# A planner's costs, seven exponential slots, and later loads in a two-layer attention and token-mixing kernel

## The chip, the cores and the metric

The kernel runs on one core of one Trainium2 chip. The metric is the device time of one execution in microseconds, the median of several runs. The profile is that of one execution; its times are counted from the first instruction of the span.

The core has five engines with a queue of instructions each: TensorE (PE) multiplies matrices and writes PSUM; VectorE (DVE), ScalarE (ACT) and GpSimd (POOL) work on tiles in SBUF and, the first two, in PSUM; SyncE (SP) issues DMAs. POOL issues two small DMAs as well. Engines wait for each other by semaphores only.

## The reference

Two kinds of blocks take turns, twice over, on x of 2048 tokens by 512 features in bfloat16.

```python
x = x + A(layernorm(x))     # attention over a sliding window
x = x + B(layernorm(x))     # a perceptron across the tokens
x = x + A(layernorm(x))
x = x + B(layernorm(x))
```

A projects to queries, keys and values (wqkv, 512 by 1536), for 32 heads of 16 features. A token attends to itself and the 255 tokens before it: scores times 1/4, masked, softmax, product with the values, and the output projection wo (512 by 512). B normalises its input once more, multiplies over the tokens with w1 (2048 by 1792), adds b1, applies the tanh form of gelu, multiplies with w2 (1792 by 2048) and adds b2. Both layers use the same weights.

## The kernel before

**Tiles.** Tokens come in 16 tiles of 128 (x_sb, and normalised xh_sb). Attention works on four quarters Q of 512 tokens. For a quarter, xhT holds the transposed normalised tokens (two buffers); k_sb, q_sb and v_all hold projections, doubled with zeros for two half sets of heads, so that small matmuls of 64 by 64 tiles can serve several heads at once. The zeros are made in `masked` (line 464 on DVE, 469 on ACT) as the projection leaves PSUM.

**Steps of attention.** A quarter has 4 groups of heads by NB = 9 shifts: 36 steps, 144 in a layer, 288 in all. A step is `emit_scores` (line 581, PE), `emit_exp` (line 592, one exponential on ACT from a pair of PSUM banks to a slot of p_sb, then one or two small multiplications with the triangles in `edge`, line 609, on POOL or DVE), and `emit_pv` (line 630, PE: the product with the values, which accumulates over the nine shifts in two PSUM banks). p_sb has NSLOT = 5 slots, taken in turn; the scores have two pairs of banks. The table `v_all` also holds ones, which make the denominators in the same product. Every second group the denominators are gathered by small DMAs into den_c, inverted (`job_inverse`), spread back over the heads by a product with the 0/1 table `spread` (`job_normalise`, line 674) and multiplied in; then comes wo (`job_outproj`, line 548) with the addition to x_sb and the statistics of the next normalisation.

**Beside the steps.** Projections (`job_k`, `job_q`, `job_v`: lines 454 and 500) of the later head groups and of the next quarter, the transposes of the next quarter, the output projection of the last quarter, and parts of the token products run between the steps of a quarter. They take their banks in turn from two (`misc_bank`). The transposes of the very first quarter are matmuls with the identity (line 443); all others are DMAs from SP (line 435).

**Token products.** `u_product` (line 752) multiplies w1 with the tokens in groups of four matmuls for each quarter of the tokens, and `job_y` (line 789) multiplies w2 in two halves of ten and four matmuls. Twelve of the sixteen output tiles of the first layer's second product are laid over the attention of the second layer.

**The order.** Nothing is ordered by hand on the engines. Every operation is entered with `plan.op`: the engines that may do it and its cost in ns on each, the resources that it reads and writes, a place `prio`, and `lat`, the time that its successors wait after its end (80 by default, 200 for PE). `Plan.arrange` walks through simulated time; an engine that is free takes, of the operations that are ready within 60 ns, the one with the lowest place (PE adds STAY = 1.0 to the place of one that would change its tile mode between "full", "columns" and "cells", and SWITCH = 100 ns to its time). A DMA ends at the end of its issue or of the bus, plus its bytes at 200 per ns, plus 1600. The order found is fixed in the program; `emit` writes it out with semaphore waits. Between two operations of PE no wait is written. Places are in units of which a quarter has 20: step n of a layer has place base + 5n/9, its scores and exponential 1.0 less, its value product 1.6 more.

**What the change touches.** `XPOS`, `XSTEP`: the places of the four loads of tokens 8 to 15 (256 KB each, tiles 8-9, 10-11, 12-13, 14-15) and, two further steps, of the two halves of wo (256 KB each); each waits by `after=latest` for the exponential that was entered last before it. `XLAT`: the additional latency of a DMA transpose. `constants`: the ones of three blocks of v_all (line 384, POOL), then spread (a memset, line 831, and sixteen selections, line 838), then the DMAs of the two bias vectors from POOL (line 844), which read spread as their time to start. `warm`: 13 groups of ten matmuls into one bank at the start (line 394). `first_norm`: the normalisation of a quarter of the input (statistics line 400, DVE; lines 408 to 420).

Of the kernel before, what the change touches and what calls it, by code (L numbers as in the profile page):

```python
# [13 lines left out]
FIRSTV = -0.7  # L14
# [5 lines left out]
XPOS = 0.7  # L20
XSTEP = 1.2
NORM0 = 6.5
XLAT = 1500
# [16 lines left out]
class Plan:  # L40
# [53 lines left out]
    def arrange(self):  # L94
# [13 lines left out]
        while todo:  # L108
# [40 lines left out]
            for s in o.succ:  # L149
                s.left -= 1  # L150
                s.ready = max(s.ready, o.end + (0 if e == "tensor" and e in s.on else o.lat))
                if not s.left:
                    for x in s.on:
                        pool[x].append(s)
# [80 lines left out]
def bass_interleave_layers__sliding_block__mixer_token_mlp__prompt_kernel(  # L235
# [20 lines left out]
    NSLOT = 5  # L256

    es = ExitStack()
    with es:
# [171 lines left out]
        def job_transpose(Q, i, prio):  # L431

            t, buf = 4 * Q + i, Q % 2
            if prio > 0:
                plan.op({SP: (600, lambda e: e.dma_start_transpose(xhT[:, buf, :, i * P:(i + 1) * P], xh_sb[:, t, :]))},
                        reads=[R("xh", t)], writes=[R("xhT", buf, i)], prio=prio, dma=1 << 17, lat=XLAT)
                return
# [21 lines left out]
        def masked(b, prio, dst, src, mask, key, writes):  # L459
# [11 lines left out]
            plan.op({ACT: (1380, each)} if key == "even" and prio < 0 else {DVE: (MASKED, both), ACT: (1380, each)}, reads=[R(key)], shares=[BK(b)], writes=writes, prio=prio)  # L471
# [37 lines left out]
        def first_jobs(p0, dp):  # L509
# [3 lines left out]
                    [(p0 + 9 + FIRSTV + 0.3 * i, lambda p, i=i: job_v(0, i, p)) for i in range(4)])  # L513

        def span_jobs(Q, p0):
# [3 lines left out]
            beside = {"q1": (0, 1), "q2": (2,), "k3": (3,)} if Q + 1 < NQ else {}  # L519
            if Q == 0:  # L520
                order = [j for j in order if j[0] != "o"]
# [162 lines left out]
        def attention(L, base):  # L684
            todo, n = [], 0
            for Q in range(NQ):
# [9 lines left out]
                todo += span_jobs(Q, base + 20 * Q)  # L696
# [114 lines left out]
        for n, a in enumerate(range(8, 16, 2)):  # L811
            todo.append((XPOS + XSTEP * n, lambda p, a=a: load_x(a, a + 2, p, after=latest)))
        for n in range(2):
            todo.append((XPOS + XSTEP * (n + 4), lambda p, n=n: load(
# [7 lines left out]
        for g in range(NQ):  # L822
            todo.append((-20 if g == 0 else 18 * g - 19, lambda p, g=g: first_norm(g, p)))

        def constants(p):
            for n in range(2, 5):
                for i in range(2):
                    put_ones(n, i, p + 5 * n, [R("xh", 3)], (POOL,))

# [21 lines left out]
        for L in range(2):  # L851
# [24 lines left out]
            for st in range(NT):  # L876
                p, b = base + 131 + st, st % 6
                if L == 0 and 4 <= st < 8:
                    p = BASE - 9 + 2.2 * (st - 4)
                elif L == 0 and st >= 8:  # L880
                    p = BASE + (8 + 3 * (st - 8) if st < 12 else 26 + 3 * (st - 12))
                    b = None
# [35 lines left out]
```

## Time and profile before

| what | value |
| --- | --- |
| median of three runs | 533.8 us (533.21 to 535.61) |
| the profiled execution | 534.36 us, its span 532.6 us |
| PE busy | 484.0 us, 91% |
| PEld (weight loads, beside PE) | 273.7 us |
| DVE, ACT, POOL busy | 318.7, 296.1, 234.4 us |
| granted TensorE clock, mean | 0.997 |
| moved by DMA | 44.38 MB, 83 GB/s |

Stages in the span: up to 13 us the first loads, normalisation and transposes; 13 to 180 us attention of layer one with parts of its first token product; 180 to 225 us the rest of that product; 225 to 248 us the first part of the second one; 248 to 437 us attention of layer two, with the rest of the second product laid over it; 437 to 530 us both token products of layer two.

How to read it: a row of the timeline has start, length, engine, line, operation, output and inputs, the number of instructions, and in brackets how long the engine was idle before and what ended that. "issue" stands where nothing that the profile shows ended it. A row of the table by stretches has, for each engine, busy time and instructions, then the granted clock of PE, the mean share of the 16 DMA engines and GB/s. A row of waits has who waited for whom, the total, the number and the longest. In the DMA view a row has a queue, its packets, MB, and the time of its packets as a share of 16 engines; packets that stand in line count while they stand, so it can pass 100%. q0 are POOL's DMAs, q1 those of SP, q8 fetches instructions.

### The profile page before, as it was taken

To read this page: it belongs to the slowest core of one execution; us is meant where nothing else is said; L and a number is where in the kernel's file an instruction comes from. 1 tells how busy PE (TensorE), PEld (TensorE's weight loads), DVE (VectorE), ACT (ScalarE), POOL (GpSimd) and SP (SyncE) were. 2 spreads that over 40 slices of the span, in tenths; PEclk is the share of its full clock that TensorE was granted. 3 is DMA by queue.
4 is the path that set the end of the run, shared out by engine and by line. 5 is a ranking of instruction groups with operands and counts; after the bars stand their busy time and mean duration, and the time that the engine had idled before them with its cause. 6 is when DMAs were issued, how large, how long until landed. Compare 5 with 4: busy or idle time off the path is not lost.

```text
span 532.6 us, 21297 instructions
## 1 busy us (share of the span) xinstructions
PE 484.0 (91%) x9540; PEld 273.7 (51%) x9618; DVE 318.7 (60%) x539; ACT 296.1 (56%) x335; POOL 234.4 (44%) x468
## 2 busy tenths in 40 slices
PE   7779889989889899999889888988998989999997
PEld 7455555655555444445545555555645544444443
DVE  5778869868767361157756767596876655221222
ACT  5757887988888304300746766479888860230000
POOL 5976864756665301101735644276565540200000
PEclk9999999999999999999999999999999999999999
DMA  6192515210135430533203410032221635053631
GB/s 198 45 121 66 103 44 97 72 45 25 45 96 158 124 108 0 138 103 78 43 3 94 105 31 25 3 53 73 83 65 57 192 113 149 1 140 97 180 113 44
DMA packets 84443, 44.38 MB, mean 83 GB/s; under 512 B 20864, under 2 KB 83328, under 8 KB 84352
## 3 DMA queue, kind: packets, MB, share of 16 engines
q1 hardware_dynamic: 80480, 43.00, 30.7%
q0 software_dynamic: 3872, 0.02, 1.9%
q8 instruction: 75, 1.23, 1.0%
q14 instruction: 16, 0.13, 0.1%
HBM read 32.51 MB, written 2.10 MB: 65 GB/s over the span
## 4 chain that ended last, share of the span: by engine, by line
PE 72%; DVE 12%; issue 7%; POOL 5%; ACT 3%; SPq 1%; DMA 0%; POOLq 0%; ACTq 0%; DVEq 0%
PE ps L789 18%; PE ps L752 18%; PE ps L581 9%; PE ps L454 8%; PE ps L630 8%; PE ps L548 5%; PE ps L500 4%; ACT p_sb L592 3%; DVE q_sb L464 2%; POOL p_sb L609 2%; DVE k_sb L464 1%; DVE xh_sb L417 1%; DVE oU L319 1%; POOL rstd L410 1%; PE ps L674 1%
## 5 line engine op out<-in xcount | busy, mean ns | idle before, releaser
L592 ACT ACTIVATE p_sb<-ps 128x1024 bf16<-128x1024 f32 (+8 forms) x288 | 261.3, 972 | 104.1 <-PE ps L581 96.3
L609 POOL TENSOR_TENSOR p_sb<-p_sb,edge 128x128 bf16<-128x128 bf16 (+2 forms) x361 | 171.8, 480 | 137.5 <-ACT p_sb L592 126.2
L581 PE MATMUL ps<-q_sb,k_sb 64*64 64x288 bf16 (+8 forms) x2816 | 106.9, 251 | 10.7 <-ACT p_sb L592 5.4
L630 PE MATMUL ps<-p_sb,v_all 64*64 64x288 bf16 (+8 forms) x2816 | 94.9, 248 | 11.1 <-POOL p_sb L609 6.0
L581 PEld LDWEIGHTS ps<-q_sb,k_sb 64*64 64x64 bf16 x2816 | 54.1, 106 | 60.5 <-ACT p_sb L592 29.7
L630 PEld LDWEIGHTS ps<-p_sb,v_all 64*64 64x64 bf16 x2816 | 58.4, 107 | 27.5 <-POOL p_sb L609 15.6
L793 DVE SCALAR_TENSOR_TENSOR x_sb<-ps,b2col,x_sb 128x512 bf16<-128x512 f32 x32 | 24.0, 750 | 76.0 <-PE ps L789 75.9
L454 PE MATMUL ps<-xhT,wqkv 128*128 128x512 bf16 x216 | 58.2, 384 | 9.8 <-issue 7.4
L789 PE MATMUL ps<-uT,w1buf 128*128 128x512 bf16 x274 | 61.8, 379 | 1.3 <-DVE rc L658 0.8
L464 DVE TENSOR_TENSOR k_sb<-ps,half 128x1024 bf16<-128x1024 f32 x32 | 39.0, 1218 | 16.1 <-PE ps L454 16.0
L752 PE MATMUL ps<-xh_sb,w1buf 128*128 128x512 bf16 x182 | 43.3, 379 | 2.0 <-issue 0.6
L400 DVE BATCH_NORM_STATS2 stats<-x_sb 128x6 f32<-128x512 bf16 x64 | 43.5, 688 | 1.1
L789 PEld LDWEIGHTS ps<-uT,w1buf 128*128 128x128 bf16 x280 | 26.8, 98 | 33.4 <-issue 1.8
L464 DVE TENSOR_TENSOR v_all<-ps,even 128x1024 bf16<-128x1024 f32 x29 | 35.1, 1217 | 11.5 <-PE ps L500 10.9
L464 DVE TENSOR_TENSOR q_sb<-ps,even 128x1024 bf16<-128x1024 f32 x31 | 37.7, 1217 | 4.5 <-PE ps L454 4.3
L410 POOL TENSOR_TENSOR rstd<-vare,mhalf 128x4 f32<-128x4 f32 x16 | 16.2, 1014 | 50.5 <-DVE nmean L412 50.4
L500 PE MATMUL ps<-wqkv,xhT 128*32 128x128 bf16 x2048 | 34.7, 220 | 3.7 <-issue 2.6
L789 PE MATMUL ps<-uT,oU 128*128 128x512 bf16 x165 | 36.8, 379 | 0.2
L454 PEld LDWEIGHTS ps<-xhT,wqkv 128*128 128x128 bf16 x256 | 20.5, 98 | 30.3 <-issue 7.8
L500 PEld LDWEIGHTS ps<-wqkv,xhT 128*32 128x32 bf16 x2048 | 29.1, 97 | 9.9 <-issue 7.2
L779 ACT ACTIVATE uT<-ps,b1col 128x512 bf16<-128x512 f32 x20 | 13.3, 689 | 36.8 <-PE ps L752 36.8
L548 PE MATMUL ps<-wo_sb,oT 128*128 128x512 bf16 x117 | 29.9, 380 | 2.9 <-DVE oT L681 1.7
(67 smaller groups left out, 396.2 us busy)
## 6 DMA issues: line engine op xcount, KB each, us to landing
w1buf<-in_B_w_dram SPq DMA_DIRECT2D x10, 896.0 KB
oU<-in_B_w_dram SPq DMA_DIRECT2D x6, 896.0 KB
w1buf<-in_B_w_dram SPq DMA_DIRECT2D x10, 512.0 KB
oU<-o SPq DMA_DIRECT2D x16, 256.0 KB
k_sb<-in_B_w_dram SPq DMA_DIRECT2D x16, 256.0 KB
xhT<-in_B_w_dram SPq DMA_DIRECT2D x8, 256.0 KB
q_sb<-in_B_w_dram SPq DMA_DIRECT2D x8, 256.0 KB
out_dram<-x_sb SPq DMA_DIRECT2D x16, 128.0 KB
```

Source lines behind the costliest of these rows:

```text
L400: dve(lambda e: e.bn_stats(stats[:, t, :], x_sb[:, t, :]), 690, prio, reads=[R("x", t)], writes=[R("stats", t)])
L454: last = e.matmul(ps[:, b, :], lhsT=wqkv[:, c, c0:c0 + P], rhs=xhT[:, buf, c, :], start=(c == 0), stop=(c == 3))
L464: return e.tensor_tensor(dst, src.unsqueeze(2).to_broadcast([P, n, 2, w]), mask[:].unsqueeze(1).unsqueeze(3).to_broadcast([P, n, 2, w]), o ...
L500: last = e.matmul(acc[32 * a:32 * a + 32, k], lhsT=xhT[:, buf, c, t0:t0 + 32], rhs=wv[:, c, :, a, :], start=(k == 0 and c == 0), stop=(k = ...
L548: last = e.matmul(ps[:, b, :], lhsT=oT[:, buf, t, i * P:(i + 1) * P], rhs=wo_sb[:, t, :], start=(t == 0), stop=(t == 3))
L581: last = e.matmul(ps[64 * c:64 * c + 64, 2 * half + r, 32 * i0:32 * i1], lhsT=k_sb[rows, ring, t, kb % 16, :], rhs=q_sb[rows, t, c, 32 * i ...
L592: latest[0] = plan.op({ACT: (170 + int(2 * (512 - c0) * 0.84), lambda e: e.activation(p_sb[:, slot, :, c0:512], ps[:, 2 * half:2 * half + ...
L609: return e.tensor_tensor(v, v, g, op=ALU.mult)
L630: last = e.matmul(ps[64 * r:64 * r + 64, B_O + (c ^ r), 32 * i0:32 * i1], lhsT=v_all[rows, col:col + 64], rhs=p_sb[rows, slot, r, 32 * i0: ...
L752: r = e.matmul(ps[:, b, :], lhsT=blk[:, n, (ft % 2) * P:(ft % 2 + 1) * P], rhs=xh_sb[:, 4 * g + n, :], start=(first and g == quarters[0] a ...
L789: r = e.matmul(ps[:, b, :], lhsT=blk[:, fc, (st % 2) * P:(st % 2 + 1) * P], rhs=uT[:, fc, :], start=(fc == 0), stop=(fc == NFT - 1))
L793: dve(lambda e: e.scalar_tensor_tensor(x_sb[:, st, :], ps[:, b, :], b2col[:, st:st + 1], x_sb[:, st, :], op0=ALU.add, op1=ALU.add), 750, prio,
```

## The change

- The loads of tokens 8 to 15 get the places 4, 9, 14, 20 (before 0.7, 1.9, 3.1, 4.3), the halves of wo 17 and 23 (before 5.5 and 6.7).
- In the walk, the successors of a PE operation now wait its latency of 200 ns on PE too; before they waited none there.
- NSLOT goes from 5 to 7.
- A DMA transpose costs SP 1230 ns in the plan (before 600), and its additional latency of 1500 goes; the common 80 stays.
- In `constants`, spread and the biases get a place 10 later (SPREADP).
- Constants become names: FIRSTV, VACT, NORM1, YP and ORDER1 have the values that stood in the code before, or leave a branch unused.

```diff
--- before.py
+++ after.py
@@ -11,16 +11,21 @@
 P = 128
 EARLY = 1.0
 PV_LAG = 1.6
-FIRSTV = -0.7
+FIRSTV = (-0.7, -0.4, -0.1, 0.2)
+VACT = 0
+NORM1 = -1
+SPREADP = 10
+ORDER1 = None
+BES1 = {"q3": (0, 1, 2, 3)}
+YP = ((-9, 2.2), (8, 3), (26, 3))
 WARM = 13
 NPART = 4
 PARTQ = (0, 1)
 UP0, UPD = 0.5, 5.0
 MASKED = 1215
-XPOS = 0.7
-XSTEP = 1.2
+XPOS = (4, 9, 14, 20)
+WOPOS = (17, 23)
 NORM0 = 6.5
-XLAT = 1500
 SPAN0 = 0.3
 SPAN = 19.0
 
@@ -148,7 +153,7 @@
             todo -= 1
             for s in o.succ:
                 s.left -= 1
-                s.ready = max(s.ready, o.end + (0 if e == "tensor" and e in s.on else o.lat))
+                s.ready = max(s.ready, o.end + o.lat)
                 if not s.left:
                     for x in s.on:
                         pool[x].append(s)
@@ -253,7 +258,7 @@
     NFT = F // P
     EPS = 1e-5
     SMSCALE = 1.0 / math.sqrt(DH)
-    NSLOT = 5
+    NSLOT = 7
 
     es = ExitStack()
     with es:
@@ -432,8 +437,8 @@
 
             t, buf = 4 * Q + i, Q % 2
             if prio > 0:
-                plan.op({SP: (600, lambda e: e.dma_start_transpose(xhT[:, buf, :, i * P:(i + 1) * P], xh_sb[:, t, :]))},
-                        reads=[R("xh", t)], writes=[R("xhT", buf, i)], prio=prio, dma=1 << 17, lat=XLAT)
+                plan.op({SP: (1230, lambda e: e.dma_start_transpose(xhT[:, buf, :, i * P:(i + 1) * P], xh_sb[:, t, :]))},
+                        reads=[R("xh", t)], writes=[R("xhT", buf, i)], prio=prio, dma=1 << 17)
                 return
             b = misc_bank()
             pv = ps[:, b, :].bitcast(dt.bfloat16)
@@ -468,7 +473,7 @@
                 for h in range(2):
                     last = e.activation(dst[:, :, h], src, ACTF.Copy, scale=mask[:, h:h + 1])
                 return last
-            plan.op({ACT: (1380, each)} if key == "even" and prio < 0 else {DVE: (MASKED, both), ACT: (1380, each)}, reads=[R(key)], shares=[BK(b)], writes=writes, prio=prio)
+            plan.op({ACT: (1380, each)} if key == "even" and prio < VACT else {DVE: (MASKED, both), ACT: (1380, each)}, reads=[R(key)], shares=[BK(b)], writes=writes, prio=prio)
 
         def job_k(Q, t, prio):
 
@@ -510,13 +515,16 @@
 
             jobs = [lambda p, i=i: job_transpose(0, i, p) for i in range(4)] + [lambda p: job_k(0, 0, p), lambda p: job_q(0, 0, p)]
             return ([(p0 + dp * n, job) for n, job in enumerate(jobs)] +
-                    [(p0 + 9 + FIRSTV + 0.3 * i, lambda p, i=i: job_v(0, i, p)) for i in range(4)])
-
-        def span_jobs(Q, p0):
+                    [(p0 + 9 + FIRSTV[i], lambda p, i=i: job_v(0, i, p)) for i in range(4)])
+
+        def span_jobs(Q, p0, L):
 
 
             order = ["k1", "q1", "v0", "v1", "k2", "q2", "v2", "o0", "k3", "q3", "o1", "v3", "K0", "Q0", "o2", "o3"]
             beside = {"q1": (0, 1), "q2": (2,), "k3": (3,)} if Q + 1 < NQ else {}
+            if L == 1 and ORDER1:
+                order = ORDER1.split()
+                beside = {} if Q + 1 == NQ else BES1
             if Q == 0:
                 order = [j for j in order if j[0] != "o"]
             if Q == NQ - 1:
@@ -693,7 +701,7 @@
                         todo.append((p0, step))
                         todo.append((p0 + PV_LAG, lambda p, a=(Q, t, m, n % NSLOT): emit_pv(*a, p)))
                         n += 1
-                todo += span_jobs(Q, base + 20 * Q)
+                todo += span_jobs(Q, base + 20 * Q, L)
             end = base + 20 * NQ
             todo.append((end + 3, lambda p: job_inverse(NQ - 1, p)))
             for t in range(2):
@@ -808,10 +816,10 @@
         BASE = 400
         todo = []
 
-        for n, a in enumerate(range(8, 16, 2)):
-            todo.append((XPOS + XSTEP * n, lambda p, a=a: load_x(a, a + 2, p, after=latest)))
+        for p0, a in zip(XPOS, range(8, 16, 2)):
+            todo.append((p0, lambda p, a=a: load_x(a, a + 2, p, after=latest)))
         for n in range(2):
-            todo.append((XPOS + XSTEP * (n + 4), lambda p, n=n: load(
+            todo.append((WOPOS[n], lambda p, n=n: load(
                 wo_sb[:, 2 * n:2 * n + 2], A_wo.rearrange("(fc p) e -> p fc e", p=P)[:, 2 * n:2 * n + 2], 1 << 18, p, after=latest,
                 writes=[R("wo", n)])))
 
@@ -820,12 +828,13 @@
                 ln_stats(t, p)
             ln_apply(g, False, p)
         for g in range(NQ):
-            todo.append((-20 if g == 0 else 18 * g - 19, lambda p, g=g: first_norm(g, p)))
+            todo.append((-20 if g == 0 else 18 * g - 18 + NORM1, lambda p, g=g: first_norm(g, p)))
 
         def constants(p):
             for n in range(2, 5):
                 for i in range(2):
                     put_ones(n, i, p + 5 * n, [R("xh", 3)], (POOL,))
+            p += SPREADP
 
 
             setup(lambda e: e.memset(spread[:], 0.0), 530, reads=[R("xh", 3)], writes=[R("spread")], prio=p)
@@ -875,11 +884,10 @@
                         todo.append((base + 126, lambda p, n=n, i=i: put_ones(n, i, p, engines=(POOL,), writes=[R("v", n, i, h) for h in range(2)])))
             for st in range(NT):
                 p, b = base + 131 + st, st % 6
-                if L == 0 and 4 <= st < 8:
-                    p = BASE - 9 + 2.2 * (st - 4)
-                elif L == 0 and st >= 8:
-                    p = BASE + (8 + 3 * (st - 8) if st < 12 else 26 + 3 * (st - 12))
-                    b = None
+                if L == 0 and st >= 4:
+                    p0, dp = YP[st // 4 - 1]
+                    p = BASE + p0 + dp * (st % 4)
+                    b = None if p >= BASE else b
                 todo.append((p, lambda p, st=st, b=b, L=L: job_y(st, misc_bank() if b is None else b, L, p)))
         todo.sort(key=lambda v: v[0])
         for p, job in todo:
```

## The prediction

> **What bounds the kernel now.** The page comes first: who is busy, and which chain ends last.
>
> ```profile
> span 532.6 us, 21297 instructions
> PE 484.0 (91%) x9540; PEld 273.7 (51%) x9618; DVE 318.7 (60%) x539; ACT 296.1 (56%) x335; POOL 234.4 (44%) x468
> ...
> PE 72%; DVE 12%; issue 7%; POOL 5%; ACT 3%; SPq 1%; DMA 0%; POOLq 0%; ACTq 0%; DVEq 0%
> ```
>
> TensorE is the bound: 484.0 of 532.6 us. The change takes no matrix work away, so all it can win lies in the other 48.6 us, and in clock lost after long pauses. The table by stage says where these are: the two long token products (180 to 248 and 437 to 530 us) are full to within 2 us, the first 13 us miss 2.6, the end 2.9; the rest, some 41 us, is holes in the two attention stages. "issue" on the chain (7%) is the largest kind: waits that no semaphore explains. The longest is in the first layer; the table of engine time by microsecond shows it (PE first, then weight loads, DVE, ACT, POOL; after them the granted clock):
>
> ```profile
> 33.00:34.00 1.00, 1.00 (x37) 0.83 (x40) 1.00 (x2) 0.93 (x2) 0.85 (x3) 1.00 7.54 12
> ...
> 37.00:38.00 1.00, 0.00 (x0) 0.00 (x0) 0.39 (x1) 0.00 (x0) 0.43 (x2) 1.00 0.53 170
> 38.00:39.00 1.00, 0.00 (x0) 0.00 (x0) 0.00 (x0) 0.00 (x0) 0.00 (x0) 1.00 0.07 14
> 39.00:40.00 1.00, 0.76 (x2) 0.13 (x2) 0.00 (x0) 0.00 (x0) 0.00 (x0) 0.58 0.00 1
> 40.00:41.00 1.00, 1.00 (x17) 0.67 (x20) 0.68 (x1) 0.10 (x1) 0.00 (x0) 0.50 0.07 16
> ```
>
> All engines stand, and the clock falls to half. In the timeline PE stops between two matmuls of one projection, where the code has no wait at all:
>
> ```profile
> 36.28 0.38 PE L454 MATMUL ps<-xhT,wqkv 128*128 128x512 bf16 x1 [0.16 <-issue]
> 39.24 1.04 PE L454 MATMUL ps<-xhT,wqkv 128*128 128x512 bf16 x2 [2.58 <-issue]
> ```
>
> So PE lacked instructions, not data. The DMA view agrees. From 31 to 36.5 us there is no packet of the instruction queue q8, but these:
>
> ```profile
> q0 software_dynamic: 3819, 0.02, 184.2%
> q1 hardware_dynamic: 729, 0.69, 59.8%
> ```
>
> and in 36.5 to 39 us one of q8:
>
> ```profile
> q8 instruction: 1, 0.02, 2.8%
> ```
>
> q0 carries the two bias vectors as 3,872 tiny packets; q1 carries tokens 12 to 15 and wo, which SP issued from 29.0 to 33.4 us. One block of instructions came late behind both.
>
> Next POOL's timeline from 18 to 29 us. It is never idle after 19.7, and every second entry builds the table spread:
>
> ```profile
> 22.95 0.39 POOL L838 TENSOR_SCALAR_AFFINE_SELECT spread<-spread 128x128 bf16<-128x128 bf16 x1
> 23.32 0.33 POOL L609 TENSOR_TENSOR p_sb<-p_sb,edge 128x64 bf16<-128x64 bf16 x1
> 23.60 0.35 POOL L838 TENSOR_SCALAR_AFFINE_SELECT spread<-spread 128x128 bf16<-128x128 bf16 x1
> ```
>
> Last the waits over the whole span (total us, times, longest):
>
> ```profile
> ACT p_sb L592 <- PE ps L630: 5.8, 6, 1.5
> ...
> PE ps L630 <- POOL p_sb L609: 6.0, 17, 1.0
> ...
> PE ps L581 <- ACT p_sb L592: 5.4, 18, 0.5
> ```
>
> The first is an exponential waiting for one of the five slots; the others are PE waiting for masks and for exponentials. They are short.
>
> **The change part by part.** The sum goes against the profiled execution, 534.36 us (span 532.6); the median of the runs is 533.8, 0.56 lower. FIRSTV, VACT, NORM1, YP and ORDER1 at their values give the same places as before: nothing.
>
> *Start.* The walk now puts 200 ns between two PE operations that depend on each other. The 13 warm-up groups write one bank, so the planned warm-up grows by 12 x 0.2 = 2.4 us, and some groups fall behind the first transposes. On the chip no wait goes with it. PE warms from 1.43 to 10.56 us (0.70 per group) and the first transpose starts at 10.40, though the first normalised tile was ready at about 8.96 (half of DVE's pair that begins at 8.59). Won at most 1.4; lost at most one group put ahead of the first projection, 0.7. I take -0.8: the fourth tile is only ready at 9.80, so not all of 1.4 comes through.
>
> *POOL and DVE from 13 to 28 us.* Spread's 17 steps get 10 units more, so the masks go first. Eleven of its steps lie after 19 us: 11 x 0.35 = 3.9 us. Tokens 8 and 9 come later too, and take their statistics (1.27 + 0.3 us) off DVE at 25.7. PE's waits in 13 to 26 us that are neither the start nor instructions are 0.9 + 0.5 + 0.5 + 0.3 + 0.2 = 2.4. But the first product with values waits for the last value tile, which DVE copies at 23.41 after the normalisation; spread is not in that chain. So a third: -0.8. Bounds: -2.4, and +1.3 if one bias issue (1.31 us on POOL) now stands before the masks.
>
> *The stall at 36.66.* Loads wait for exponentials 7, 16, 25 and 35 (x) and 30 and 41 (wo), instead of 1 to 12. Counted in the trace these end at about 27.5, 35.1, 48, 56, 52 and 61 us. So 1 MB leaves the stretch around 33, and the biases, behind spread, go some microseconds later. The stall costs 2.58 us; the half clock after it makes the 16 + 16 score and value matmuls take 1.04 + 0.96 where 0.54 + 0.49 is seen at 44.5, and two projections about 0.7 more: 0.97 + 0.7 = 1.7. Together 4.3. The tiny packets stay, and the 1.01 us stall at 73.38 shows what one block of instructions costs beside a single 0.5 MB load. I take 4.3 - 1.0: -3.3. Bounds -4.3 and 0. [...]
>
> *Where the moved loads are needed.* Tokens 14 and 15 land near 59 us; the normalisation of their group runs on DVE and POOL at 65 to 70. wo lands near 64 and is first read at 82.07 (line 548). Price 0, hidden behind exponentials; without that cover PE would wait the difference, about 3 us. On SP nothing urgent stands behind these loads: the transposes of the second quarter get free of four loads at 26.5 to 31.8, those at 55.0 may get a load before them (0.4 us).
>
> *Seven slots.* The scores of a step are placed 2.6 units before its values, 4.7 steps, so five slots bind now and then and seven do not. Bounds: 0, and -5.8 (all of ACT's wait). From 62 to 142 us PE is busy 71.9 and ACT 67.9 of 80, so most of ACT's wait is covered by PE: a quarter, -1.5.
>
> *PE's latency elsewhere.* Two value products that follow each other are now parted in the plan by whatever else is ready, often a filler (projection 0.87, half of a token product up to 2.17 us). On the chip the work is the same; each added change from 64x64 to full tiles costs 0.16 us (the gap before most L454). Bounds: -2, if scores come forward to ACT, and +7.7, if one step in six of the 288 gets a change more. I take +0.4, two or three changes: the walk had such choices before. In the long token products chains interleave, but PE waits for nothing there: 0; if a gelu became the last thing before the second product, one ACTIVATE, 0.69.
>
> *Transposes.* SP is now charged 1230 ns (the trace: 1238 median) and nothing above the common latency, so the planned landing comes 4.36 - 3.57 = 0.8 us earlier. The first user is planned 1.2 units, some 2.6 us, behind. No wait row of PE shows a late one today. 0; with the cover gone 0.8 for each of 6 groups, 4.7.
>
> Sum: -0.8 - 0.8 - 3.3 - 1.5 + 0.4 = -6.0: 528.4 on the profiled scale, 527.8 against the median.
>
> **The rivals.** *The order gets worse.* With 39 changes of 0.16 us on the chain now, 48 more cost 7.7. In 102 to 112 us ACT is busy 9.77 of 10, so a score that a filler delays is not caught up there. From 38 added changes on, the 6.0 above are eaten; with the early gains at half (-3.0) and all 7.7 lost it ends at 538.5. For it: nearly every value product depends on the one before. Against: PE must do the fillers anyway, and each needs one of two banks and a DVE copy of 1.2 us first.
>
> *The stall moves.* The biases, issued some microseconds later, meet the next block as they do now; only the small terms remain, and seven slots win nothing: 533.8 - 1.6 + 0.4 = 532.6, within what can be told. For it: the 3,872 packets stay, and a block is due about every 4 us. Against: from 36 us on, the megabyte beside them moved at 200 to 340 GB/s until the block came, and it is gone.
>
> *Instructions arrive ahead anyway.* If a deep store of instructions hides the block and PE stood for something else, the 4.3 stay as they are and the rest gives 533.8 - 2.7 = 531.1. [...] Against it: no row names another cause, and PE stood inside one operation.
>
> **How the numbers follow.** The forecast has 0.58, the worse order 0.27, the moved stall 0.10, the hidden block 0.05. Measurements of this kernel lie 533.2 to 535.6 us, so about 0.5% (2.7 us) can be told from no change. Faster takes nearly all of the forecast and half of the last: 0.60; the same 0.15 (the moved stall and rest); slower 0.25. The forecast's own range is 522.5 to 531: below lie the lower ends of start, POOL and stall with half of the slots' 5.8 (1.4 + 2.4 + 4.3 + 2.9 = 11.0, 522.8). The full range reaches into the worse order, to 540.
>
> **What would show it.** PE without a pause over 1.2 us from 30 to 45 us, and clock 1.00 there; x and wo issues single, from 27 to 62 us; masks ahead of spread from 19 us; the first transpose near 9.5; ACT's wait for L630 gone; 0.16 us changes to full tiles on the chain still about 40. It is wrong if PE's holes from 62 to 180 and 260 to 437 us grow by more than 3 us, or a stall over 2 us stands beside the bias packets.

## The result and the profile after

The changed kernel takes 537.49 us (median of 20 runs, 532.56 to 542.48); the kernel before, beside it, 534.34 us (20 runs, 533.21 to 536.2). The ratio is 1.0049, 95% interval 1.0032 to 1.0066: slower by half a per cent, where 1.1% faster (6.0 us) was forecast. The runs of the changed kernel spread over 10 us, those before over 3; that spread turns out to be part of the answer. The longest, 542.48 us, counts as a slow run and stands outside the ratio.

The profiled execution of the changed kernel took 539.37 us, its span 537.6 us, its mean granted clock 0.990 (before 0.997). First the page of the kernel after: busy times, then the chain by engine.

```profile
span 537.6 us, 21374 instructions
PE 498.1 (93%) x9618; PEld 276.9 (51%) x9618; DVE 318.2 (59%) x541; ACT 297.7 (55%) x337; POOL 234.3 (44%) x465
...
PE 77%; DVE 7%; issue 5%; POOL 4%; ACT 4%; DMA 1%; SPq 0%; POOLq 0%; ACTq 0%; DVEq 0%
```

PE's busy time seems to have grown by 14 us, but no matrix work was added. Read the counts first: before, 9,540 matmuls stand beside 9,618 weight loads; after, 9,618 beside 9,618. The profile of before lacks 78 records of matmuls, and what they took is missing from its busy time. Busy PE can't be compared between these two; the starts of the exponentials can.

The stretch that was to gain, in the table by stretches of the kernel after (PE, PEld, DVE, ACT, POOL; granted clock; DMA share; GB/s), with two later stretches:

```profile
32.00:38.00 6.00, 5.93 (x177) 3.57 (x168) 5.25 (x7) 4.84 (x8) 5.00 (x13) 1.00 1.14 52
38.00:44.00 6.00, 5.92 (x173) 3.72 (x167) 5.86 (x10) 4.82 (x8) 4.83 (x14) 1.00 0.29 79
56.00:62.00 6.00, 3.79 (x80) 2.19 (x79) 3.77 (x5) 2.42 (x4) 2.00 (x3) 0.79 0.76 87
...
300.00:310.00 10.00, 7.68 (x228) 5.11 (x220) 5.45 (x12) 8.29 (x9) 7.13 (x12) 0.83 0.33 80
360.00:370.00 10.00, 7.83 (x200) 4.76 (x192) 7.21 (x9) 5.82 (x7) 5.37 (x10) 0.83 0.29 86
```

From 32 to 44 us PE is full and the clock whole: the stall of 2.58 us and its half clock are gone. Now PE loses 2.2 of 6 us at 56 us and 2.2 to 2.3 of 10 at 300 and 360 us, and in each the clock falls. Before, it was halved once, at 39.2 us; here three times, at 59.5, 305.3 and 366.7 us. What this does to the lead is seen in the starts of the exponentials, counted in both traces (us):

| exponential | before | after | after - before |
| --- | --- | --- | --- |
| 0 | 17.74 | 17.94 | +0.20 |
| 9 | 28.80 | 27.24 | -1.56 |
| 18 | 40.90 | 36.07 | -4.83 |
| 27 | 49.67 | 43.89 | -5.78 |
| 36 | 56.98 | 52.14 | -4.84 |
| 45 | 67.01 | 66.09 | -0.92 |
| 63 | 88.89 | 87.44 | -1.45 |
| 144 (first of layer two) | 252.85 | 252.71 | -0.14 |
| 189 | 310.19 | 310.25 | +0.06 |
| 198 | 322.50 | 325.39 | +2.89 |
| 225 | 364.80 | 368.92 | +4.12 |
| 252 | 393.90 | 399.88 | +5.98 |
| 287 (last) | 433.20 | 438.13 | +4.93 |

The forecast gain of some 6 us is there by exponential 27. It is given back in two places: nearly four of the 5.8 us between 52 and 66 us, and six from 310 to 400 us.

The first place in PE's timeline of the kernel after:

```profile
55.26 0.84 PE L505 MATMUL ps<-wqkv,xhT 128*32 128x128 bf16 x45
58.31 0.46 PE L505 MATMUL ps<-wqkv,xhT 128*32 128x128 bf16 x19 [2.21 <-issue]
58.70 0.41 PE L589 MATMUL ps<-q_sb,k_sb 64*64 64x128 bf16 x12
59.05 1.49 PE L459 MATMUL ps<-xhT,wqkv 128*128 128x512 bf16 x4
```

This is the old stall at a new place: PE stops within one projection, for 2.21 us, for nothing that a semaphore explains. The next projection takes 1.49 us where 1.02 was seen at 11.85: half clock. SP's timeline ahead of it and the DMA view of 53 to 56 us (packets, MB, share of 16 engines) show what the block of instructions met:

```profile
52.52 0.54 SPq L318 DMA_DIRECT2D w1buf<-in_B_w_dram  x1
53.16 0.53 SPq L318 DMA_DIRECT2D x_sb<-in_A_x_dram  x1
53.77 2.52 SPq L440 DMA_TRANSPOSE xhT<-xh_sb  x2
```

```profile
q1 hardware_dynamic: 1208, 0.60, 69.6%
q8 instruction: 1, 0.02, 2.2%
```

The one packet of q8 starts at 55.89, when PE has 0.2 us of instructions left, and takes 1.07 us; PE is back 1.35 us after its end. Counted back 128.5 weight loads from the stall (the spacing of such stalls, counted further down), PE entered the block before it at 53.65, so the fetch started 2.25 us after that. The same at 71.5 us: a w1 load of 512 KB issued at 68.07, the packet 2.69 us after the block was entered, and a stall of 2.12 us. PE ate these two blocks, by that count some 128 weight loads with their matmuls each, in 2.5 and 2.9 us.

The waits of PE in the kernel after (total us, times, longest):

```profile
PE ps L589 <- issue: 7.8, 7, 2.1
PE ps L589 <- ACT p_sb L600: 7.4, 19, 0.7
PE ps L505 <- issue: 4.4, 6, 2.2
PE ps L638 <- POOL p_sb L617: 3.9, 12, 0.6
PE ps L638 <- issue: 2.3, 2, 1.3
PE ps L638 <- DVE o L324: 2.3, 5, 0.9
```

Waits for masks fell from 6.0 to 3.9 us, those for exponentials rose from 5.4 to 7.4, and "issue", read here as lack of instructions, is the largest kind with 14.5 us.

### The profile page after: what moved, and what is told of

Read it like the earlier page. It is cut to its first block, busy times and chain, and to the rows that moved or that the text cites. A ratio compares the mean times of both kernels' runs of the same rounds, so it can differ in the third digit from the quotient of the medians.

```text
span 537.6 us, 21374 instructions
## 1 busy us (share of the span) xinstructions
PE 498.1 (93%) x9618; PEld 276.9 (51%) x9618; DVE 318.2 (59%) x541; ACT 297.7 (55%) x337; POOL 234.3 (44%) x465
## 3 DMA queue, kind: packets, MB, share of 16 engines
q0 software_dynamic: 3872, 0.02, 1.1%
## 4 chain that ended last, share of the span: by engine, by line
PE 77%; DVE 7%; issue 5%; POOL 4%; ACT 4%; DMA 1%; SPq 0%; POOLq 0%; ACTq 0%; DVEq 0%
PE ps L760 18%; PE ps L797 18%; PE ps L589 11%; PE ps L638 9%; PE ps L459 9%; PE ps L556 6%; PE ps L505 5%; ACT p_sb L600 4%; POOL p_sb L617 2%; DMA oU<-o 1%; PE ps L682 1%; DVE o L324 1%; DVE q_sb L469 1%; DVE stats L405 1%; POOL rstd L415 1%
## 5 line engine op out<-in xcount | busy, mean ns | idle before, releaser
L617 POOL TENSOR_TENSOR p_sb<-p_sb,edge 128x256 bf16<-128x256 bf16 (+2 forms) x357 | 169.8, 480 | 141.9 <-ACT p_sb L600 131.6
L589 PE MATMUL ps<-q_sb,k_sb 64*64 64x288 bf16 (+8 forms) x2816 | 111.8, 252 | 15.9 <-issue 7.8
L638 PE MATMUL ps<-p_sb,v_all 64*64 64x288 bf16 (+8 forms) x2816 | 107.0, 252 | 10.5 <-POOL p_sb L617 3.9
L589 PEld LDWEIGHTS ps<-q_sb,k_sb 64*64 64x64 bf16 x2816 | 56.1, 107 | 59.9 <-ACT p_sb L600 33.3
L638 PEld LDWEIGHTS ps<-p_sb,v_all 64*64 64x64 bf16 x2816 | 60.4, 109 | 33.3 <-POOL p_sb L617 17.0
L459 PE MATMUL ps<-xhT,wqkv 128*128 128x512 bf16 x256 | 67.1, 387 | 1.7 <-DVE v_all L469 0.7
L797 PE MATMUL ps<-uT,w1buf 128*128 128x512 bf16 x280 | 63.6, 379 | 0.0
L760 PE MATMUL ps<-xh_sb,w1buf 128*128 128x512 bf16 x192 | 45.4, 380 | 0.1
L469 DVE TENSOR_TENSOR k_sb<-ps,half 128x1024 bf16<-128x1024 f32 x31 | 37.6, 1214 | 8.0 <-PE ps L459 7.9
L797 PE MATMUL ps<-uT,oU 128*128 128x512 bf16 x168 | 36.7, 379 | 0.0
L556 PE MATMUL ps<-wo_sb,oT 128*128 128x512 bf16 x128 | 32.3, 381 | 0.5 <-DVE oT L689 0.5
```

What stands on the lines that cost most here:

```text
L459: last = e.matmul(ps[:, b, :], lhsT=wqkv[:, c, c0:c0 + P], rhs=xhT[:, buf, c, :], start=(c == 0), stop=(c == 3))
L469: return e.tensor_tensor(dst, src.unsqueeze(2).to_broadcast([P, n, 2, w]), mask[:].unsqueeze(1).unsqueeze(3).to_broadcast([P, n, 2, w]), o ...
L556: last = e.matmul(ps[:, b, :], lhsT=oT[:, buf, t, i * P:(i + 1) * P], rhs=wo_sb[:, t, :], start=(t == 0), stop=(t == 3))
L589: last = e.matmul(ps[64 * c:64 * c + 64, 2 * half + r, 32 * i0:32 * i1], lhsT=k_sb[rows, ring, t, kb % 16, :], rhs=q_sb[rows, t, c, 32 * i ...
L617: return e.tensor_tensor(v, v, g, op=ALU.mult)
L638: last = e.matmul(ps[64 * r:64 * r + 64, B_O + (c ^ r), 32 * i0:32 * i1], lhsT=v_all[rows, col:col + 64], rhs=p_sb[rows, slot, r, 32 * i0: ...
```

## The experiments

Each run was compared with the kernel before on the same chip; "times" are medians, ratios carry 95% intervals. Two theories at first: the loads, moved, now collide elsewhere; or the order got worse through the latency rule.

### Each part alone

On the kernel before, only the new places of the loads:

```diff
-XPOS = 0.7
-XSTEP = 1.2
+XPOS = (4, 9, 14, 20)
+WOPOS = (17, 23)
...
-            todo.append((XPOS + XSTEP * n, lambda
+            todo.append((p0, lambda
```

> The kernel before with the new places of the x and wo loads alone. Blocks theory (PE stands where a block of instructions is fetched beside heavy loads, and the clock halves after it): the stall of 2.6 us near 37 us goes, and 3 to 5 us are won up to exponential 27; whether they are kept depends on the next load that meets a block: 529 to 534. Order theory (the loads are innocent, the new order of PE is what costs): faster by 3 to 5 us to the end, about 530.

537.06 us, ratio 1.0051 [1.0028, 1.0075]: slower, alone, and outside what either theory expected. PE and DVE in its timelines, then SP's:

```profile
70.30 0.41 PE L581 MATMUL ps<-q_sb,k_sb 64*64 64x192 bf16 x10
72.74 0.20 PE L581 MATMUL ps<-q_sb,k_sb 64*64 64x32 bf16 x2 [2.04 <-issue]
...
94.73 0.41 PE L630 MATMUL ps<-p_sb,v_all 64*64 64x288 bf16 x8 [2.15 <-DVE agg L401]
```

```profile
93.89 0.69 DVE L319 COPY o<-ps 128x512 f32<-128x512 f32 x1 [2.91 <-DMA oU<-o]
```

```profile
88.99 0.40 SPq L313 DMA_DIRECT2D w1buf<-in_B_w_dram  x1
89.48 0.73 SPq L313 DMA_DIRECT2D oU<-o  x1
```

The stall at 36.7 us is gone here too (0.36 us left), and exponential 27 comes 1.97 us earlier. Then PE stops twice. The first stop, 2.04 us with half clock at 73.8 us after it, stands at the block of instructions where the kernel before lost 1.01 us. The second, of 2.15 us, is no lack of instructions: the transfer of o2 to oU is issued behind a 512 KB w1 load on SP and lands 0.6 us after it, at 93.77 us; DVE waits 2.91 us for it before it can empty a value bank again, and PE for DVE. No moved load is issued in the 5 us before either stop; the order around them changed. From exponential 72 on the kernel is 0.9 to 2.4 us late.

On the kernel before, spread and the biases ten later:

```diff
                     put_ones(n, i, p + 5 * n, [R("xh", 3)], (POOL,))
+            p += 10
```

> The kernel before with spread and the biases 10 places later, alone. Blocks theory: the megabyte of x and wo stays together with the bias packets, so a stall of about 2.5 us stays between 33 and 42 us, and the rest is a microsecond at most: 533 to 535. Rival (the tiny packets alone make the stall): it moves with the bias packets and keeps its length; also 533 to 535, but the stall lies beside them wherever they are.

531.54 us, 0.9951 [0.9929, 0.9973]: faster. The megabyte of x and wo stayed where it was (issued from 28.4 to 33.2 us), the biases moved (issued at 31.43 and 33.15 us, before at 28.85 and 30.17), and no stall over 1 us stands near 37 us. Both theories had expected one. Taking either the megabyte or the biases away removes the stall. The other traces agree: at this block PE stands for instructions 1.49 to 3.13 us in all five kernels that keep both (before, s_lat, s_slots, s_transp, q_before) and at most 0.4 us in the other twelve.

On the kernel before, only the latency:

```diff
-                s.ready = max(s.ready, o.end + (0 if e == "tensor" and e in s.on else o.lat))
+                s.ready = max(s.ready, o.end + o.lat)
```

> The kernel before with the 200 ns between dependent operations of PE in the walk, alone. Order theory: this is what loses, 3 to 6 us, nearly all of it in the attention of the second layer (exponentials 190 to 250) and 1.2 us at its start, where two halves of the token products end together: 537 to 540. Blocks theory: 533 to 537, with the loss only where a new stall on a block boundary stands.

537.09 us, 1.0048 [1.0024, 1.0072]: slower. That lies where the two expected ranges meet and doesn't tell the theories apart.

The slots (`NSLOT = 5` to `7`) and the transposes (600 to 1230, no XLAT), each alone:

> The kernel before with seven slots alone. By the prediction's term -1.5 us: 531 to 533 where before is 532 to 534, ACT's wait for line 630 gone. Rival (the plan hardly needs more than five slots): no change within 0.2%.

530.11 us, 0.9957 [0.994, 0.9974]: faster.

> The kernel before with the new transpose costs alone (1230 ns on SP, no additional latency). By the prediction 0; PE waits for no late transpose. Rival: the earlier planned landing makes PE wait up to 0.8 us at each of six groups, up to 4.7 us slower.

531.45 us, 0.9984 [0.9959, 1.0009]: no difference.

The product of the five ratios is 0.999, all five together gave 1.0049. The parts don't add.

### Parts taken out of the changed kernel

The old latency rule; the old places of the loads; and both, which leaves spread, slots and transposes:

```diff
-                s.ready = max(s.ready, o.end + o.lat)
+                s.ready = max(s.ready, o.end + (0 if e == "tensor" and e in s.on else o.lat))
```

```diff
-XPOS = (4, 9, 14, 20)
-WOPOS = (17, 23)
+XPOS = (0.7, 1.9, 3.1, 4.3)
+WOPOS = (5.5, 6.7)
```

> The changed kernel with the old latency rule in the walk (none between PE operations). Order theory: 530 to 532, the early gain is kept and the loss in the second layer goes. Blocks theory: no better than 534, as long as a stall near 56 us and one in the second layer remain.

> The changed kernel with the x and wo loads at their old, early places. Loads theory (the new places put x and wo beside the first-layer weight loads, the transposes and the o2 transfer, and cost about 3 us as they did alone): 533 to 535. Order theory (only the latency rule costs): 537 to 539, since the early stall is not there once the biases are late.

> The changed kernel with old load places and the old latency rule: what is left is spread 10 later, seven slots and the new transpose costs. If both the loads and the latency rule lose on their own: 526.5 to 529, better than 529.7 with the new loads. If the loads gain once the rule is gone: 530 to 533. No PE pause over 2 us and no half clock in the span.

| ratio to before | new loads | old loads |
| --- | --- | --- |
| new latency | 1.0049 [1.0032, 1.0066] (after) | 1.0017 [0.9993, 1.0041] (u_loads) |
| old latency | 0.9912 [0.988, 0.9944] (u_lat) | 0.9944 [0.9923, 0.9966] (keep3) |

The latency rule costs 1.4% of the time beside the new loads, 0.7% beside the old ones. The loads seem to cost 0.3% beside the new rule and to gain 0.3% beside the old, though in both rows the intervals overlap. In keep3's profile one half clock is left, at 59.3 us, where none was expected. Without the rule the changed kernel takes 529.70 us, close to the forecast. The rule is the term that turned the sign. Each theory has one run on its side: u_lat came where the order theory had it, 0.3 us under its 530 to 532, and u_loads, at 533.65 us, within the loads theory's 533 to 535.

Half of the rule at a time, after operations on full tiles or after "cells" alone:

```diff
-                s.ready = max(s.ready, o.end + o.lat)
+                s.ready = max(s.ready, o.end + (0 if e == "tensor" and e in s.on and o.mode == "cells" else o.lat))
```

```diff
-                s.ready = max(s.ready, o.end + o.lat)
+                s.ready = max(s.ready, o.end + (0 if e == "tensor" and e in s.on and o.mode != "cells" else o.lat))
```

> The changed kernel, where the walk counts 200 ns between dependent PE operations only after full-tile and column operations (warm-up, projections, both token products), not after 64x64 ones (scores, value products). If the cost comes from chains of token products that end together and hold their banks longer: 535 to 538. If it comes from parting value products: 529 to 532.

> The other half: 200 ns counted only after 64x64 operations (scores, value products, the spreading of the inverses). If parting the value products costs: 535 to 538. If the chains of token products cost: 529 to 532. If neither alone does, both kernels lie near 530 and the cost is in single stalls that the order happens to hit.

l_full 531.99 us, 0.9988 [0.9968, 1.0008]; l_cells 533.60 us, 1.0006 [0.999, 1.0023]. Against u_lat (0.9912) the halves cost 0.8% and 0.9%, the whole rule 1.4%. Neither kind of operation carries it alone.

### Smaller neighbours for the instruction blocks

If the stalls at 56 and 71 us are blocks behind 512 KB, halved loads should take them away. Each w1 load becomes two of 256 KB, the second placed halfway to the next load:

```diff
-        def w1_half_dma(fb, h, prio):
-            load(w1buf[:, fb, 8 * h:8 * h + 8, :], w1v[:, 8 * h:8 * h + 8, fb * 256:(fb + 1) * 256], 1 << 19, prio, after=latest,
+        def w1_half_dma(fb, h, prio, j):
+            s = slice(8 * h + 4 * j, 8 * h + 4 * j + 4)
+            load(w1buf[:, fb, s, :], w1v[:, s, fb * 256:(fb + 1) * 256], 1 << 18, prio, after=latest,
...
-                            todo.append((base + (12 + 7 * (2 * k + h) if L == 0 else 42 + 6 * (2 * k + h)), lambda p, k=k, h=h: w1_half_dma(k, h, p)))
+                            todo.append((base + (12 + 7 * (2 * k + h) + 3.5 * j if L == 0 else 42 + 6 * (2 * k + h) + 3 * j),
+                                         lambda p, k=k, h=h, j=j: w1_half_dma(k, h, p, j)))
```

On the changed kernel, on the changed kernel with the old latency, and on the kernel before:

> The changed kernel, where each 512 KB load of w1 is issued as two of 256 KB, half a distance apart. Blocks theory: the blocks of instructions near 56 and 71 us come earlier, both stalls of 2.1 to 2.2 us shrink below 1.2, and the half clock at 59 goes: about 3 us less than the changed kernel up to exponential 45, the second layer unchanged; ratio to before about 1.000. Rival (those stalls come from the rate at which PE eats instructions, not from the loads): no change, ratio 1.005.

> The changed kernel with the old latency rule and the halved w1 loads. If the first-layer stalls left in it (1.7 us at 71) come from the loads: ratio to before 0.988 or lower, the fastest so far. If not: 0.991 as without the halving.

> The kernel before with each 512 KB load of w1 as two of 256 KB, alone. Blocks theory: the stall at 36.7 stays (bias packets and the megabyte of x and wo, not w1), the 1.0 us at 73.4 goes: ratio 0.996 to 1.000. If the halving is worth the same 0.9% everywhere: 0.991.

The changed kernel goes to 530.38 us, 0.9960 [0.9942, 0.9977]; with the old latency 527.78 us, 0.9905 [0.9882, 0.9928], the fastest of all, though against 0.9912 without the halving the intervals overlap, so by its own expectation the loads are not shown to cost there; the kernel before stays at 532.68 us, 1.0001 [0.9981, 1.0021]. The stretches of q_after:

```profile
56.00:62.00 6.00, 5.45 (x251) 4.48 (x256) 4.27 (x9) 4.57 (x6) 5.22 (x9) 1.00 0.41 113
62.00:72.00 10.00, 7.94 (x303) 5.26 (x298) 7.49 (x13) 8.46 (x10) 6.61 (x12) 1.00 0.43 74
```

The stalls at 56 and 71 us are gone and the clock is whole. But one caution: the planner reacts to every entry. In q_after 1,772 of PE's 9,618 weight loads stand at another place than in after, so its 0.9% against after (0.9960 to 1.0049) is the loads and a new order together; its profile also has half clock from 299.7 to 306.6 us. In q_before all engines but SP keep exactly their order, so it is the clean test. There the old stall stays, with a w1 load half the size, while the stall at 74 us, where the load is w1's, shrinks from 1.01 to 0.46 us. PE in q_before, then the last place in before:

```profile
36.35 0.60 PE L454 MATMUL ps<-xhT,wqkv 128*128 128x512 bf16 x2
39.19 0.60 PE L454 MATMUL ps<-xhT,wqkv 128*128 128x512 bf16 x2 [2.23 <-issue]
...
74.00 0.38 PE L500 MATMUL ps<-wqkv,xhT 128*32 128x128 bf16 x13 [0.46 <-issue]
```

```profile
74.38 0.38 PE L500 MATMUL ps<-wqkv,xhT 128*32 128x128 bf16 x13 [1.01 <-issue]
```

That agrees with an old stall made by the biases and the megabyte of x and wo, not by w1, and a second one made by w1. The second block (left between 69 and 78 us) shows it across the traces: in the eleven kernels where a 512 KB w1 load is issued 0.6 to 1.1 us before PE enters the block ahead of it, the packet comes 1.8 to 3.1 us after that entry and PE stands 1.0 to 2.5 us; in s_spread, where no such load is near, the packet comes after 0.64 us and PE does not stand.

### A pause for data

From 302 to 305 us PE's pauses in the changed kernel are not instructions. PE, then DVE:

```profile
302.63 0.41 PE L589 MATMUL ps<-q_sb,k_sb 64*64 64x128 bf16 x12 [0.52 <-ACT p_sb L600]
303.55 0.41 PE L589 MATMUL ps<-q_sb,k_sb 64*64 64x160 bf16 x12 [0.50 <-ACT p_sb L600]
304.46 0.41 PE L589 MATMUL ps<-q_sb,k_sb 64*64 64x192 bf16 x12 [0.50 <-ACT p_sb L600]
305.68 1.09 PE L638 MATMUL ps<-p_sb,v_all 64*64 64x288 bf16 x20 [0.80 <-DVE o L324]
```

```profile
302.33 0.68 DVE L324 COPY oU<-ps 128x512 f32<-128x512 f32 x1
302.93 1.42 DVE L422 TENSOR_SCALAR xh_sb<-x_sb,rstd,shift 128x512 bf16<-128x512 bf16 x2
304.27 0.74 DVE L617 TENSOR_TENSOR p_sb<-p_sb,edge 128x256 bf16<-128x256 bf16 x1
304.94 0.68 DVE L324 COPY o<-ps 128x512 f32<-128x512 f32 x1
```

Two normalisations and a mask got between the two copies that empty the value banks; scores can go on only as far as exponentials do, and values wait. The copies were put eight places earlier, on q_after and q_ulat:

```diff
-                copy_out(oU[:, buf, t, :], ps[:, B_O, :], B_O, prio, 680, held_o(buf, t))
-                copy_out(o2[:, k, :], ps[:, B_O + 1, :], B_O + 1, prio, 680, [R("o2", k)])
+                copy_out(oU[:, buf, t, :], ps[:, B_O, :], B_O, prio - 8, 680, held_o(buf, t))
+                copy_out(o2[:, k, :], ps[:, B_O + 1, :], B_O + 1, prio - 8, 680, [R("o2", k)])
```

> The changed kernel with halved w1 loads, and the two copies that free the value banks placed 8 units earlier. If the rest of the latency rule's cost is the bank that waits near 300 us (0.8 us of wait, 1.5 of waits for exponentials before it, and the half clock after it): ratio 0.991 to 0.993. If the order as a whole costs: 0.996 as without the edit.

> The same edit without the latency rule, on the fastest kernel so far (0.9905). The banks there hold no long wait: 0.988 to 0.992.

e_after 530.72 us, 0.9957 [0.994, 0.9974], as q_after without the edit; e_ulat 531.29 us, 0.9966 [0.9947, 0.9986], slower than q_ulat. That is also outside what was expected of it. The clock loss did fall, from 1.6 to 0.4 half-clock stretches of 3.41 us per run by the mean clocks, but other waits of 1.2 to 1.5 us stand in e_after's profile (60.6, 98.3, 110.3 and 147.7 us). So this pause alone doesn't explain what the latency rule costs. What it costs in q_after against q_ulat, 0.55%, is not settled: the order as a whole differs.

## Why the prediction was wrong, step by step

**The stall at 36.66** (-3.3): right at its place, and even too small: from exponential 9 to 18 the lead grows by 3.3 us and to 27 by 4.2. Each of two edits alone removes it. What failed is the silent assumption that a gain at 36 us stays until the end. The rival "the stall moves" had it half: stalls of that size came, though not with the biases. In the kernel after the tiny packets of q0 are transferred from 31.9 to 35.9 us (before 33.0 to 36.9, so they did not come later, as the working had it), and the block fetched among them, between 33 and 34 us, delays nothing. The new stalls stand at the w1 loads of 52.5 and 68.1 us, which had been there all the time. The working had called a 1.01 us stall beside a 0.5 MB load "what one block costs"; at that same block it is now 2.12 us, and with transposes and another load beside it 2.21 at 56 us.

**Where the moved loads are needed** (0): the step that failed first, in part. It asked who needs x and wo, and when, and that was right: the six loads go out one by one in the order given, from 27.5 to 62.6 us, and nobody waits for them. (wo is read first at 78.64 us in before, not at 82.07; the price stays 0.) It didn't ask what they meet on the queue and on the DMA engines. A load of x issued at 53.16 stands between a 512 KB w1 load and two transposes, and a block is due there. That the load of x adds to what the w1 load does there is argued from its place: in u_loads, with the old places, PE does not stand at this block, but there its order differs too. That "nothing urgent stands behind these loads" on SP held: the chain of the kernel after passes o2's transfer twice, but loads of B's weights stand ahead of it, not moved ones, and DVE waits only 0.8 us for the two together. Both, with some of the longest pieces of "issue", in that chain:

```profile
42.87 3.80 DMA oU<-o
56.10 2.21 issue
71.59 2.12 issue
...
256.81 1.41 issue
...
364.26 1.83 issue
408.26 4.09 DMA oU<-o
```

Alone, the loads' new places cost 0.5% (2.7 us), where the working had 0 for them and -3.3 for the stall.

**PE's latency elsewhere** (+0.4): the step that failed and decides the sign. Measured: 2.6 us alone (0.48% of 534), some 7 us in the changed kernel (1.0049 against 0.9912). Its upper bound of 7.7 held that, but for a wrong reason. The price of 0.16 us for each change to full tiles was no cost: before most L454 the profile of before lacks one of four matmuls, and the gap is where its record should be. The lines shown ahead have x1 and x2 for a projection of four. In q_before, which runs the same order on PE with all records there, the 31 gaps are one, the old stall. PE's waits in before and in q_before:

```profile
PE ps L454 <- issue: 7.4, 31, 2.6
```

```profile
PE ps L454 <- issue: 2.2, 1, 2.2
```

PE is busy for 496.6 us there, so some 12.6 of the 48.6 us in which the prediction saw room were matmuls too. So "0.16 us changes about 40" could be neither right nor wrong, and the rival "the order gets worse" ended on the right side with a mechanism that doesn't exist. From exponential 189 to 252, in layer two, the kernel falls 5.9 us back. The prediction called itself wrong if holes grew by over 3 us; two stretches of half clock, estimated at half of their 6.8 us, make up 3.4 of the 5.9, so whether the holes alone did is not told. What the runs show in place of the mode changes is less tidy: both halves of the rule cost, and each place seen is a lost lead or a pause of another kind. One is the start of layer two: before, four matmuls of y run after the K projection (249.53 us), and the copy of K starts on an idle DVE; after, y is complete earlier, but its last addition and DVE's statistics stand ahead of the copy of K.

```profile
248.19 0.73 DVE L801 SCALAR_TENSOR_TENSOR x_sb<-ps,b2col,x_sb 128x512 bf16<-128x512 f32 x1
248.84 1.22 DVE L469 TENSOR_TENSOR k_sb<-ps,half 128x1024 bf16<-128x1024 f32 x1
```

That copy starts at 248.84, before at 248.87: a lead of 1.2 us at y's start (223.45 against 224.66) is gone. Why the whole of the order costs what it does stays open.

**Missing from the sum: the clock as multiplier.** The 1.7 us of half clock were counted once, for the stall that goes, not for any that comes. In the runs of the kernel after, time follows the mean clock: 532.56 us at 1.000, 540.26 at 0.987. A stretch of 3.41 us at half takes 0.0032 off the mean, and a line through the 19 runs that count gives 533.0 us with none and 1.6 us for each (correlation 0.85). The mean is 2.3 stretches per run; in the runs of the kernel before beside the experiments, 27 to 35 on each of four chips, it is 0.4 to 0.8. The difference of 1.5 to 1.9 stretches is worth 2.4 to 3.0 us, most of the 3.15 that the medians differ by. It does not explain the whole miss: with no half clock at all the line still gives 533.0, some 5 us above the forecast. And this is a fit, not an edit. u_lat and q_ulat have 0.3 and 0.0 stretches per run, s_lat and s_loads 2.5 and 1.6, which agrees; l_full has 2.4 and is as fast as the kernel before, which does not.

**Start** (-0.8): the first transpose came at 9.05 (before 10.40) and the first projection at 11.85 (13.16), as worked out; yet exponential 0 starts at 17.94, before at 17.74. What is late next was not named: a group of warm-up stands at 12.71 between the K and Q projections, and ACT empties four value tiles first.

```profile
15.49 2.56 ACT L474 ACTIVATE v_all<-ps,even 128x512 bf16<-128x512 f32 x4
17.94 1.89 ACT L600 ACTIVATE p_sb<-ps 128x1024 bf16<-128x1024 f32 x2
```

The lead comes through later: 1.0 us at exponential 2, 1.6 at exponential 9. It belongs to the latency rule. In all five other traces in which the rule holds for full tiles exponential 9 comes 1.4 to 1.7 us earlier than before, 1.48 in s_lat; in the ten without it at most 0.12. So this part won about 1.5, twice its term and a little over its bound of 1.4.

**POOL and DVE from 13 to 28 us** (-0.8): masks do go ahead of spread, but the lead at exponential 9 is that of the start. In s_spread alone exponential 9 is 0.11 us later, and the wait of 0.9 us of the first product with values, which the profile of before puts down to spread, is still 0.9 us there, now put down to the last value tile, as the working had feared. Up to there the term won nothing; that the two terms' sum of -1.6 fits the lead is luck.

**Seven slots** (-1.5): -0.43% alone, 2.3 us, and ACT's wait for the value products falls from 5.8 to 1.6 us there (in the kernel after it is no longer among the rows of waits). The number fits, but how much of it the slots made is not shown: 2.2 us of the lead in that trace come between exponentials 9 and 27, where the old stall is 1.49 us and no half clock follows. **Transposes** (0): no difference, right.

**Instructions arrive ahead anyway**: wrong. Each packet of q8 has 16,384 bytes, and weight loads between such stalls come in multiples of about 128.5 (386 for three packets from 58.31 to 73.71 us, 1,156 for nine from there to 113.65), each with its matmul; over the whole span of the kernel after 75 packets stand beside 9,618 weight loads, one for 128. The fetch is not hidden here: in the attention stages of the kernel after most packets (40 of 67) start 0.3 to 1.2 us after PE entered the block before, take 0.9 to 1.4 us, and where PE stands for them it is back 1.3 to 1.5 us after their end. Added up, as an estimate from these three, 2.5 to 4.1 us go by from one block to the next, and a block that PE ate faster than the next one came made it stand even beside an idle DMA: the one entered at 254.23 us was eaten in 2.6, PE went on 4.0 us after that entry, and at 256.81 us, in the chain shown above, 1.41 us are lost with no other transfer begun in the 4 us before. The other stalls for "issue" of over 1 us in layer two (1.14, 1.26 and 1.83 us) stand at such borders as well.

## What to carry to other kernels

A stall that is taken out early is a lasting gain only if the work that comes forward meets nothing: list the transfers and the blocks of instructions that each earlier microsecond will now run into, not only the users of what was moved. Price a pause of an engine whose granted clock falls at its length plus the half clock that follows (here 3.41 us of it, after single pauses of 1.8 to 2.6 us in before and after), and look at the clock of every run: here the kernel with more such pauses also spread more from run to run. Before a small, regular gap in a trace becomes a price, count the records of both kernels' instructions; a missing record looks like an idle engine. And credit a lead to a part only when a run with that part alone has it: here two terms fitted one lead, and one of them had made it.

## What the runs showed of the hardware

The half clock (granted 0.50) lasts 3.41 us, or twice that (6.83 us in q_after and s_transp). In the kernel after the granted clock changes at 59.50, 62.91, 305.26, 308.67, 366.70 and 370.11 us: these lie 1, 71, 1, 17 and 1 times 3.413 us apart. Divided into such stretches, counted from these changes, the traces of before and after have half clock after those in which PE multiplied least, 0.35, 0.44 and 0.46 of the time in the kernel after, 0.22 before; the lowest share there without half clock behind it is 0.54. The pauses were single ones of 2.58 us (before), 2.21 and 1.83 us (after, at 56 and 364 us), and once four of 0.5 to 0.8 us in a row (302 to 305 us). Two pauses of like length ended differently: 2.21 us at 56 us left 0.35 of one stretch and halved the clock; 2.12 us at 71.5 us lay across the border of two, left 0.54 and 0.81, and cost only itself. The border isn't sharp: in other runs stretches of 0.50 to 0.68 were followed by half clock (in q_after one of about 0.55, from 296.3 to 299.7 us, with pauses of 0.52, 0.50 and 0.50 us), and some of 0.46 to 0.51 were not.

In these runs the small packets delayed a block of instructions much only together with other traffic. In the kernel before its packet came 3.49 us after PE entered the block ahead of it, beside 3,872 tiny packets and a megabyte; with the megabyte spread (s_loads) it came after 0.92 us, and with the biases moved (s_spread) after 0.74. A megabyte delayed one without them as well: in u_loads, with early loads and late biases, the packet came after 2.26 us, before nearly all of the tiny packets, though PE did not stand for it.
